# Chunks of 4096 rows with three buffers, evictions on ScalarE alone, weights in halves and a split store, in a 1x1 depthwise-separable convolution

## The chip, the cores and the metric

The kernel runs on one core of a Trainium2 chip. The metric is the time of one execution on the device in microseconds (us). The kernel before was timed nine times: median 589.32 us, lowest 587.19, highest 592.49.

## The reference

The input x is (1, 384, 384, 384) bf16: 147,456 pixels of 384 channels. With a depthwise kernel of size 1 the convolution is a scale of each channel, and the pointwise part is a 384 x 384 matrix product:

```python
def reference(x, dw, pw):          # dw: (1, 1, 384), pw: (384, 384)
    out = x * dw[0, 0]
    return jnp.einsum('bhwc,cd->bhwd', out, pw)
```

The kernel folds dw into the rows of pw once and then computes x times that matrix. Input and output are 113.2 MB each.

## The kernel before, in words

The pixels are 147,456 rows. 512 rows make a supertile, of which there are 288, and some supertiles make a chunk: 1, 1, 2, then 70 chunks of 4 (`LMAX`), then 2, 1, 1 (`_chunks`). A chunk is what one load or one store moves. In a chunk of L supertiles each of the 128 partitions holds 4 L consecutive rows, so a load has one contiguous run of 3072 L bytes per partition, 12 KB for L = 4. The store has four runs of 768 L bytes per partition, 3 KB for L = 4, because a quarter q of each supertile's rows comes out together. There are four X buffers (`NX`) and four O buffers (`NO`).

A supertile passes through these steps:

- VectorE (DVE) transposes it (L174). Two bf16 channels are taken as one 32-bit word, and 32 x 32 blocks are transposed, in two instructions: h = 0 for channels 0 to 191, h = 1 for the others. The result is T, in two buffers that alternate with the supertile's number.
- TensorE (PE) computes it in 48 matmuls (L134): 6 blocks b of channels, 2 parities `par`, and 4 row groups q of 32 partitions, which run side by side on the array. Each has 32 x 128 stationary values from T and streams 384 columns of the scaled weights w_r. The four q have a PSUM bank each, and PS has two sets of four, s = 0 and 1.
- The evictions go from PSUM to O as bf16: three of the four banks by ScalarE (ACT) in one instruction (L215), the fourth by VectorE (L212).
- The store goes out when the chunk is evicted.

The PE instructions are a loop of 144 passes, two supertiles each. The first matmul of a supertile waits until ACT has emptied its banks, that of q = 3 until VectorE has; each half waits for its transposes (L133 and the loop around it), and each finished half counts up `s_pe`, which the evictions and the next transposes into the same T wait for. VectorE's order is: eviction of supertile jj, then the transposes of jj + 2.

All loads and stores of x and out are issued by SyncE (SP) in one queue: first the loads of the first four chunks, then for each t load t + 4 (L95, waits until the last transpose of chunk t has read its X buffer) and store t (L105 and L107, wait for both evictions of its last supertile). An eviction into an O buffer in use waits for that store (L210, L211).

At the start ACT and SP issue dw, the first chunk and four copies of pw, one for each 32 partitions (L89). VectorE spreads dw over the partitions as dwsel (L186), transposes supertile 0, and then VectorE and ACT scale six slices of pw each, giving w_r (L197, L199). PE starts when all twelve are there. Two memsets and two tiny copies set the semaphores of the PSUM banks to "free".

Of the kernel before, what the change touches and what calls it, by code (L numbers as in the profile page):

```python
# [7 lines left out]
BF16 = mybir.dt.bfloat16  # L8
F32 = mybir.dt.float32
U32 = mybir.dt.uint32  # L10
COPY = mybir.ActivationFunctionType.Copy

LMAX = 4
NX = 4
NO = 4


def _chunks(n_super: int):

    head, tail = [1, 1, 2], [2, 1, 1]  # L20
    mid = n_super - sum(head) - sum(tail)
    assert mid > 0 and mid % LMAX == 0
    return head + [LMAX] * (mid // LMAX) + tail


@with_exitstack
def kernel(
# [11 lines left out]
    nc = tc.nc  # L39
    P = nc.NUM_PARTITIONS  # L40
    B, H, W, C = x.shape
    assert dw.shape[0] == 1 and dw.shape[1] == 1, "only k=1 depthwise supported"
    D = pw.shape[1]
    N = B * H * W
    assert C == 384 and D == 384 and N % 1024 == 0
    NB = C // 64

    xf = x.rearrange("b h w c -> (b h w) c")
    of = out.rearrange("b h w d -> (b h w) d")

    NS = N // 512
    chunks = _chunks(NS)
    NT = len(chunks)
    s0 = [sum(chunks[:t]) for t in range(NT)]

    consts = ctx.enter_context(tc.tile_pool(name="consts", bufs=1))
# [3 lines left out]
    pw_r = consts.tile([P, NB, 2, D], BF16, name="pw_r")  # L60
    w_r = consts.tile([P, NB, 2, D], BF16, name="w_r")
    dwt = consts.tile([32, NB, 2], BF16, name="dwt")
    dwsel = consts.tile([P, NB * 2], F32, name="dwsel")
    warm = consts.tile([P, 3], F32, name="warm")
    seed = consts.tile([P, 2], F32, name="seed")

    Xs = [bufp.tile([P, 4 * LMAX, C], BF16, name=f"X{i}") for i in range(NX)]
    Ts = [bufp.tile([P, NB, 256], BF16, name=f"T{i}") for i in range(2)]
    Os = [bufp.tile([P, 4 * LMAX * D], BF16, name=f"O{i}") for i in range(NO)]
# [3 lines left out]
    s_t = [[nc.alloc_semaphore(f"s_t{i}{h}") for h in range(2)] for i in range(2)]  # L73
    s_pe = nc.alloc_semaphore("s_pe")
    s_a = [nc.alloc_semaphore(f"s_a{i}") for i in range(2)]
    s_d = [nc.alloc_semaphore(f"s_d{i}") for i in range(2)]
    s_o = [nc.alloc_semaphore(f"s_o{i}") for i in range(NO)]
    s_dw = nc.alloc_semaphore("s_dw")
    s_pw = nc.alloc_semaphore("s_pw")
    s_ds = nc.alloc_semaphore("s_ds")  # L80
    s_wr = nc.alloc_semaphore("s_wr")
    s_seed = nc.alloc_semaphore("s_seed")

    with tc.tile_critical():  # L84
        pw_v = pw.rearrange("(b w r) d -> w b (r d)", w=32, r=2)
        dw_v = dw.rearrange("a e (b w r) -> w (a e b) r", w=32, r=2)

        def load_pw(eng, q):
            eng.dma_start(pw_r[32 * q : 32 * q + 32].rearrange("w b r d -> w b (r d)"), pw_v).then_inc(s_pw, 16)  # L89

        def load_x(t):
            L = chunks[t]
            r = 512 * s0[t]
            src = xf[r : r + 512 * L, :].rearrange("(p s) c -> p (s c)", p=P)
            d = nc.sync.dma_start(Xs[t % NX][:, : 4 * L, :].rearrange("p s c -> p (s c)"), src)  # L95
            if t >= NX:
                je = s0[t - NX] + chunks[t - NX] - 1
                d._wait_ge(s_t[je % 2][1], je // 2 + 1)
            d.then_inc(s_x[t % NX], 16)

        def store(t):
            L = chunks[t]
            r = 512 * s0[t]
            je = s0[t] + L - 1
            nc.sync.wait_ge(s_d[je % 2], je // 2 + 2)  # L105
            dst = of[r : r + 512 * L, :].rearrange("(q p j) d -> p q (j d)", q=4, p=P)
            d = nc.sync.dma_start(dst, Os[t % NO][:, : 4 * L * D].rearrange("p (q e) -> p q e", q=4))  # L107
            d._wait_ge(s_a[je % 2], je // 2 + 2)
            d.then_inc(s_o[t % NO], 16)


        nc.scalar.dma_start(dwt[:], dw_v).then_inc(s_dw, 16)
        load_x(0)
        load_pw(nc.scalar, 2)
        load_pw(nc.sync, 0)
        load_pw(nc.scalar, 3)
        load_pw(nc.sync, 1)
        for t in range(1, NX):
            load_x(t)
        for t in range(NT):  # L120
            if t + NX < NT:
                load_x(t + NX)
            store(t)
        for o in range(NO):
            nc.sync.wait_ge(s_o[o], 16 * len(range(o, NT, NO)))


        def supertile(s, rv):
            for b in range(NB):
                for par in range(2):  # L130
                    for q in range(4):
                        if par == 0 and q == 0 and b in (0, 3):
                            nc.tensor.wait_ge(s_t[s][b // 3], rv)  # L133
                        mm = nc.tensor.matmul(  # L134
                            PS[s][:, q, :D],
                            lhsT=Ts[s][32 * q : 32 * q + 32, b, par::2],
                            rhs=w_r[32 * q : 32 * q + 32, b, par, :],
                            start=(b == 0 and par == 0),
                            stop=(b == NB - 1 and par == 1),
                            tile_position=(32 * q, 0),  # L140
                        )
                        if b == 0 and par == 0 and q == 0:
                            mm._wait_ge(s_a[s], rv)
                        elif b == 0 and par == 0 and q == 3:
                            mm._wait_ge(s_d[s], rv)
                        if b in (2, 5) and par == 1 and q == 3:
                            mm.then_inc(s_pe)

        nc.tensor.wait_ge(s_wr, 2 * NB)
        with nc.tensor.Fori(0, NS // 2, 1) as it:  # L150
            rv = nc.tensor.to_reg(it + 1)
            for s in range(2):
                supertile(s, rv)


        for s in range(2):
            nc.vector.memset(seed[:, s : s + 1], 0.0).then_inc(s_d[s])  # L157
        nc.gpsimd.memset(warm[:], 0.0).then_inc(s_seed)  # L158
        for s in range(2):
            c = nc.scalar.copy(warm[:, s + 1 : s + 2], warm[:, 0:1])  # L160
            if s == 0:
                c._wait_ge(s_seed, 1)
            c.then_inc(s_a[s])

        def transposes(t, j):
            jj = s0[t] + j
            L = chunks[t]
            s = jj % 2
            Xw = Xs[t % NX][:].bitcast(U32)[:, : 4 * L, :].rearrange("p (k l) c -> p k l c", l=L)
            Tw = Ts[s][:].bitcast(U32).rearrange("p b (i k) -> p b k i", k=4)  # L170
            for h in range(2):
                if h == 0 and j == 0:
                    nc.vector.wait_ge(s_x[t % NX], 16 * (t // NX + 1))
                ins = nc.vector.transpose(  # L174
                    out=Tw[:, 3 * h : 3 * h + 3],
                    in_=Xw[:, :, j, 96 * h : 96 * h + 96].rearrange("p k (b w) -> p b k w", w=32),
                )
                if jj >= 2:
                    ins._wait_ge(s_pe, 2 * (jj - 2) + h + 1)
                ins.then_inc(s_t[s][h])  # L180

        order = [(t, j) for t in range(NT) for j in range(chunks[t])]

        nc.vector.wait_ge(s_dw, 16)
        for q in range(4):
            nc.vector.tensor_copy(  # L186
                dwsel[32 * q : 32 * q + 32, :], dwt[:].rearrange("w b r -> w (b r)")
            ).then_inc(s_ds)
        transposes(*order[0])
        for b in range(NB):  # L190
            for r in range(2):
                eng = nc.vector if r == 0 else nc.scalar
                if b == 0:
                    eng.wait_ge(s_pw, 64)  # L194
                sc = dwsel[:, 2 * b + r : 2 * b + r + 1]
                if r == 0:
                    i = nc.vector.tensor_scalar_mul(w_r[:, b, r, :], pw_r[:, b, r, :], sc)  # L197
                else:
                    i = nc.scalar.activation(w_r[:, b, r, :], pw_r[:, b, r, :], COPY, scale=sc)  # L199
                if b == 0:  # L200
                    i._wait_ge(s_ds, 4)
                i.then_inc(s_wr)
        transposes(*order[1])

        for jj, (t, j) in enumerate(order):
            L = chunks[t]
            s = jj % 2
            Ov = Os[t % NO][:, : 4 * L * D].rearrange("p (q j d) -> p q j d", q=4, d=D)
            if j == 0 and t >= NO:
                nc.vector.wait_ge(s_o[t % NO], 16 * (t // NO))  # L210
                nc.scalar.wait_ge(s_o[t % NO], 16 * (t // NO))  # L211
            e = nc.vector.tensor_copy(Ov[:, 3, j, :], PS[s][:, 3, :D])  # L212
            e._wait_ge(s_pe, 2 * jj + 2)
            e.then_inc(s_d[s])
            a = nc.scalar.copy(Ov[:, 0:3, j, :], PS[s][:, 0:3, :D])  # L215
            a._wait_ge(s_pe, 2 * jj + 2)
            a.then_inc(s_a[s])
            if jj + 2 < NS:
                transposes(*order[jj + 2])


# [28 lines left out]
```

## Time and profile before

| what | value |
|---|---|
| median of nine runs | 589.32 us |
| profiled execution, time in all | 587.68 us |
| its span, first to last instruction | 585.9 us |
| PE busy | 563.3 us (96%) |
| DVE busy | 564.0 us (96%) |
| ACT busy | 326.7 us (56%) |
| share of the 16 DMA engines taken by SP's queue | 98.6% |
| moved | 227.81 MB, 389 GB/s over the span |
| granted TensorE clock, mean | 0.995 |
| share of the chain that ended last: PE, DMA, ACT | 93%, 4%, 1% |

The profile is one execution. Times in views of it count from the span's start. A line like L134 is a line of the kernel. "Idle before" is time in which an engine had nothing running before an instruction, put down to what released it. A transfer's time "to landing" runs from its issue to the last of the semaphore marks that its DMA engines leave, so it contains the time in which it waits behind earlier transfers.

### The profile page before, as it was taken

What the parts mean: (1) busy time and instruction counts of PE and PEld (TensorE: products, weight loads), DVE (VectorE), ACT (ScalarE), POOL (GpSimd) and SP (SyncE); (2) the same over time, 40 slices, a digit from 0 to 9 for tenths busy, and PEclk for the clock granted to TensorE, in tenths of its full rate; (3) what the DMA queues carried; (4) which work ended last, traced back from release to release, by engine and by line L of the source; (5) the groups of instructions that cost most, each with busy time, mean ns of one, the idle gap of its engine ahead of it and who ended that gap; (6) DMA issues with size and microseconds to landing.
All of it is one profiled execution on the core that took longest, in us unless ns stands there. A gap on an engine that the chain in (4) does not pass through costs nothing.

```text
span 585.9 us, 30055 instructions
## 1 busy us (share of the span) xinstructions
PE 563.3 (96%) x13824; PEld 384.9 (66%) x13824; DVE 564.0 (96%) x876; ACT 326.7 (56%) x297; POOL 0.3 (0%) x5
## 2 busy tenths in 40 slices
PE   1999999999999999999999999999999999999993
PEld 0666666666666666666666666666666666666662
DVE  3899999999999999999999999999999999999993
ACT  3555555555565656565555555555555555555552
POOL 0000000000000000000000000000000000000000
PEclk9999999999999999999999999999999999999997
DMA  8999999999999999999999999999999999999965
GB/s 284 361 414 417 412 398 391 396 397 395 408 415 403 395 403 411 398 393 407 403 407 410 412 408 393 390 403 415 407 401 390 402 384 392 419 392 387 388 243 211
DMA packets 52126, 227.81 MB, mean 389 GB/s; under 512 B 2704, under 2 KB 6544, under 8 KB 43152
## 3 DMA queue, kind: packets, MB, share of 16 engines
q1 hardware_dynamic: 51488, 227.09, 98.6%
q10 hardware_dynamic: 624, 0.59, 0.4%
q14 instruction: 13, 0.11, 0.0%
q8 instruction: 1, 0.02, 0.0%
HBM read 114.43 MB, written 113.25 MB: 389 GB/s over the span
## 4 chain that ended last, share of the span: by engine, by line
PE 93%; DMA 4%; ACT 1%; SPq 0%; issue 0%; ACTq 0%
PE ps L134 93%; DMA out_dram<-O 3%; DMA pw_r<-in_pw_dram 1%; ACT w_r L199 1%; ACT O L215 0%; SPq L89 0%; SPq L95 0%; SPq L245 0%; ACTq L211 0%; ACTq L194 0%; SPq L84 0%
## 5 line engine op out<-in xcount | busy, mean ns | idle before, releaser
L134 PE MATMUL ps<-w_r,T 32*128 32x384 bf16 x13824 | 563.3, 322 | 13.1 <-ACT w_r L199 13.1
L134 PEld LDWEIGHTS ps<-w_r,T 32*128 32x128 bf16 x13824 | 384.9, 93 | 191.1 <-issue 13.1
L215 ACT CAST O<-ps 128x1152 bf16<-128x1152 f32 x288 | 322.0, 1118 | 243.2 <-PE ps L134 242.0
L174 DVE STREAM_TRANSPOSE T<-X 128x384 uint32<-128x384 uint32 x576 | 449.6, 858 | 0.0
L212 DVE CAST O<-ps 128x384 bf16<-128x384 f32 x288 | 160.7, 558 | 6.1 <-PE ps L134 4.2
L199 ACT ACTIVATE w_r<-pw_r,dwsel 128x384 bf16<-128x384 bf16 x6 | 3.1, 603 | 5.8 <-DMA pw_r<-in_pw_dram 5.8
L186 DVE CAST dwsel<-dwt 32x12 f32<-32x12 bf16 x4 | 0.7, 164 | 3.8 <-DMA dwt<-in_dw_dram 3.7
L197 DVE TENSOR_SCALAR w_r<-pw_r,dwsel 128x384 bf16<-128x384 bf16 x6 | 1.5, 314 | 2.5 <-DMA pw_r<-in_pw_dram 2.5
L160 ACT ACT_TABLE_LOAD x1 | 1.3, 1283 | 2.3 <-issue 2.3
L157 DVE MEMSET seed<- 128x1 f32 x2 | 0.1, 59 | 1.0 <-SPq L84 1.0
L160 ACT COPY warm<-warm 128x1 f32<-128x1 f32 x2 | 0.3, 189 | 0.0
L234 POOL MEMSET const-bfloat16-1.0<- 128x1 bf16 x1 | 0.1, 101 | 0.0
L234 POOL MEMSET const-uint8-127<- 128x1 uint8 x1 | 0.1, 101 | 0.0
L158 POOL MEMSET warm<- 128x3 f32 x1 | 0.1, 100 | 0.5 <-SPq L84 0.5
L234 POOL MEMSET const-float32-0.0<- 128x1 f32 x1 | 0.1, 98 | 0.2 <-issue 0.2
L234 POOL MEMSET const-float32-1.0<- 128x1 f32 x1 | 0.1, 98 | 0.0
## 6 DMA issues: line engine op xcount, KB each, us to landing
X<-in_x_dram SPq DMA_DIRECT2D x70, 1536.0 KB, 13.7
out_dram<-O SPq DMA_DIRECT2D x70, 1536.0 KB, 15.3
X<-in_x_dram SPq DMA_DIRECT2D x4, 384.0 KB, 10.8
X<-in_x_dram SPq DMA_DIRECT2D x2, 768.0 KB, 14.0
out_dram<-O SPq DMA_DIRECT2D x4, 384.0 KB, 7.1
out_dram<-O SPq DMA_DIRECT2D x2, 768.0 KB, 9.6
pw_r<-in_pw_dram ACTq DMA_DIRECT2D x2, 288.0 KB, 6.1
pw_r<-in_pw_dram SPq DMA_DIRECT2D x2, 288.0 KB, 6.7
```

The costliest lines, as they stand in the source:

```text
L134: mm = nc.tensor.matmul(PS[s][:, q, :D], lhsT=Ts[s][32 * q : 32 * q + 32, b, par::2], rhs=w_r[32 * q : 32 * q + 32, b, par, :], start=(b = ...
L157: nc.vector.memset(seed[:, s : s + 1], 0.0).then_inc(s_d[s])
L158: nc.gpsimd.memset(warm[:], 0.0).then_inc(s_seed)
L160: c = nc.scalar.copy(warm[:, s + 1 : s + 2], warm[:, 0:1])
L174: ins = nc.vector.transpose(out=Tw[:, 3 * h : 3 * h + 3], in_=Xw[:, :, j, 96 * h : 96 * h + 96].rearrange("p k (b w) -> p b k w", w=32),)
L186: nc.vector.tensor_copy(dwsel[32 * q : 32 * q + 32, :], dwt[:].rearrange("w b r -> w (b r)")).then_inc(s_ds)
L197: i = nc.vector.tensor_scalar_mul(w_r[:, b, r, :], pw_r[:, b, r, :], sc)
L199: i = nc.scalar.activation(w_r[:, b, r, :], pw_r[:, b, r, :], COPY, scale=sc)
L212: e = nc.vector.tensor_copy(Ov[:, 3, j, :], PS[s][:, 3, :D])
L215: a = nc.scalar.copy(Ov[:, 0:3, j, :], PS[s][:, 0:3, :D])
L234: nc = _bacc.Bacc("TRN2", target_bir_lowering=False, num_devices=1)
```

## The change

- `LMAX` goes from 4 to 8, and X and O have three buffers each instead of four. The chunks become 1, 1, 2, 2, 3, 3, 4, then 32 of 8, then 6, 4, 3, 2, 1. A full chunk's load has runs of 24 KB, its store runs of 6 KB.
- In every fourth full chunk (t = 9, 13, ... 37) the store is issued as four transfers: partitions 0 to 111, 112 to 118, 119 to 125 and 126 to 127.
- ACT evicts all four banks (L256 of the changed kernel), and VectorE none, except in the very last supertile, where each takes two banks, and SP and ACT store one half each. The matmul of q = 3 no longer waits for VectorE, and the two memsets go.
- The weights are loaded in eight transfers, blocks 0 to 2 of all partitions first, then 3 to 5. dwsel is made by ACT. VectorE scales nine of the twelve slices, ACT three (par = 1 of b = 0, 2, 4). PE no longer waits for all twelve: in supertiles with s = 0 the first matmul of each (b, par) waits for its own slice.
- Before its first supertile PE runs 88 matmuls on a tile of zeros, which POOL fills; their result is overwritten.

```diff
-LMAX = 4
-NX = 4
-NO = 4
+LMAX = 8
+NX = 3
+NO = 3
...
-    head, tail = [1, 1, 2], [2, 1, 1]
+    head, tail = [1, 1, 2, 2, 3, 3, 4], [6, 4, 3, 2, 1]
...
+        parts = {t: [(0, P)] for t in range(NT)}
+        for t in range(NT):
+            if chunks[t] == LMAX and t % 4 == 1:
+                parts[t] = [(0, 112), (112, 119), (119, 126), (126, 128)]
...
-            nc.sync.wait_ge(s_d[je % 2], je // 2 + 2)
             dst = of[r : r + 512 * L, :].rearrange("(q p j) d -> p q (j d)", q=4, p=P)
-            d = nc.sync.dma_start(dst, Os[t % NO][:, : 4 * L * D].rearrange("p (q e) -> p q e", q=4))
-            d._wait_ge(s_a[je % 2], je // 2 + 2)
-            d.then_inc(s_o[t % NO], 16)
+            src = Os[t % NO][:, : 4 * L * D].rearrange("p (q e) -> p q e", q=4)
+            nc.sync.wait_ge(s_a[je % 2], je // 2 + 2)
+            for lo, hi in parts[t]:
+                nc.sync.dma_start(dst[lo:hi], src[lo:hi]).then_inc(s_o[t % NO], 16)
...
         load_x(0)
-        load_pw(nc.scalar, 2)
-        load_pw(nc.sync, 0)
-        load_pw(nc.scalar, 3)
-        load_pw(nc.sync, 1)
+        for h in range(2):
+            for q in range(2):
+                load_pw(nc.scalar, 2 + q, h)
+                load_pw(nc.sync, q, h)
         for t in range(1, NX):
             load_x(t)
-        for t in range(NT):
+        for t in range(NT - 1):
             if t + NX < NT:
                 load_x(t + NX)
             store(t)
+        nc.sync.dma_start(of_last[:, 2:4], o_last[:, 2:4])._wait_ge(s_d, 1).then_inc(
+            s_last, 16
+        )
...
+        wr_eng = {(b, r): int(r == 1 and b % 2 == 0) for b in range(NB) for r in range(2)}
...
                         if b == 0 and par == 0 and q == 0:
                             mm._wait_ge(s_a[s], rv)
-                        elif b == 0 and par == 0 and q == 3:
-                            mm._wait_ge(s_d[s], rv)
+                        elif s == 0 and q == 0:
+                            mm._wait_ge(*wr_done[b, par])
...
-        nc.tensor.wait_ge(s_wr, 2 * NB)
+        nc.tensor.wait_ge(s_zero, 1)
+        with nc.tensor.Fori(0, 11, 1) as _:
+            for i in range(8):
+                nc.tensor.matmul(
+                    PS[1][:, i % 4, :D],
+                    lhsT=zero[32 * (i % 4) : 32 * (i % 4) + 32, 0:P],
+                    rhs=zero[32 * (i % 4) : 32 * (i % 4) + 32, :],
+                    start=True,
+                    stop=True,
+                    tile_position=(32 * (i % 4), 0),
+                )
+        nc.tensor.wait_ge(*wr_done[0, 0])
...
-        nc.vector.wait_ge(s_dw, 16)
+        nc.scalar.wait_ge(s_dw, 16)
         for q in range(4):
-            nc.vector.tensor_copy(
-                dwsel[32 * q : 32 * q + 32, :], dwt[:].rearrange("w b r -> w (b r)")
-            ).then_inc(s_ds)
+            nc.scalar.copy(dwsel[32 * q : 32 * q + 32, :], dwt[:].rearrange("w b r -> w (b r)")).then_inc(s_ds)
...
-            e = nc.vector.tensor_copy(Ov[:, 3, j, :], PS[s][:, 3, :D])
-            e._wait_ge(s_pe, 2 * jj + 2)
-            e.then_inc(s_d[s])
-            a = nc.scalar.copy(Ov[:, 0:3, j, :], PS[s][:, 0:3, :D])
+            nq = 4
+            if jj + 1 == NS:
+                nq = 2
+                nc.vector.wait_ge(s_o[t % NO], o_count[t % NO][t // NO])
+                e = nc.vector.tensor_copy(Ov[:, nq:4, j, :], PS[s][:, nq:4, :D])
+                e._wait_ge(s_pe, 2 * jj + 2)
+                e.then_inc(s_d)
+            a = nc.scalar.copy(Ov[:, 0:nq, j, :], PS[s][:, 0:nq, :D])
             a._wait_ge(s_pe, 2 * jj + 2)
             a.then_inc(s_a[s])
             if jj + 2 < NS:
                 transposes(*order[jj + 2])
+        nc.scalar.dma_start(of_last[:, 0:2], o_last[:, 0:2])._wait_ge(s_a[(NS - 1) % 2], (NS - 1) // 2 + 2).then_inc(
+            s_last, 16
+        )
```

## The prediction, made before the changed kernel was run

> **What bounds the kernel now.** I read four views: the page's groups of instructions, the chain that ended last, the transfers by window, and the busy table of chosen windows. First the groups (line, engine, operation, tiles, shape, count; then busy us, mean ns of one, idle us before them and who ended it):
>
> ```profile
> L134 PE MATMUL ps<-w_r,T 32*128 32x384 bf16 x13824 | 563.3, 322 | 13.1 <-ACT w_r L199 13.1
> L215 ACT CAST O<-ps 128x1152 bf16<-128x1152 f32 x288 | 322.0, 1118 | 243.2 <-PE ps L134 242.0
> L174 DVE STREAM_TRANSPOSE T<-X 128x384 uint32<-128x384 uint32 x576 | 449.6, 858 | 0.0
> L212 DVE CAST O<-ps 128x384 bf16<-128x384 f32 x288 | 160.7, 558 | 6.1 <-PE ps L134 4.2
> ```
>
> PE and VectorE both look full. The start times decide. Matmuls start in groups of four every 162.5 ns, 12 groups a supertile, and supertiles 1.950 us apart, at every percentile from the 5th to the 99th, with no longer step where a wait stands (b = 0, b = 3). ACT and DVE evictions start within 0.01 us of each other, so both are released by PE. VectorE fits (0.48 us from eviction to transposes, 1.48 us back) with nothing spare, but PE never waits for it. So between the second supertile and the last PE sets a pace that no edit here changes: 288 x 1.950 = 561.6 us. Time can be won only before and after it. The chain shows both (start us, us, what):
>
> ```profile
> 1.89 7.70 DMA pw_r<-in_pw_dram
> ...
> 9.67 3.15 ACT w_r L199 x6
> ...
> 13.15 547.73 PE ps L134 x12779
> ...
> 562.04 14.82 DMA out_dram<-O
> ...
> 576.93 1.12 ACT O L215
> ```
>
> Head: the weights land at 9.58, ACT scales its six slices, PE starts at 13.15. Its first 10 groups take 320 ns, the others 162.5: 10 x 157.5 ns = 1.5 us lost, and the second supertile starts at 16.62, the third at 18.57. Tail: the last matmul ends at 576.44 and the span at 585.9, so 9.5 us follow; a store that took 14.82 us delays the last eviction by some 0.4 us of them. That store needs explaining. Time from issue to landing, from 100 to 150 us and then from 500 to 550:
>
> ```profile
> out_dram<-O SPq DMA_DIRECT2D x7, 1536.0 KB, 11.7
> X<-in_x_dram SPq DMA_DIRECT2D x6, 1536.0 KB, 10.5
> ```
>
> ```profile
> out_dram<-O SPq DMA_DIRECT2D x7, 1536.0 KB, 21.2
> X<-in_x_dram SPq DMA_DIRECT2D x5, 1536.0 KB, 20.1
> ```
>
> The same transfers take 9.5 us longer. Each leaves 16 landing marks, one per DMA engine. For the store issued at 109.6 us the 15th mark came after 11.3 us and the last after 11.4; for that of 538.6, after 11.4 and 21.7. One engine lags by 10.3 us in 430, 2.4%; fifteen keep up. The busy table at the end (window, length, PE, PEld, DVE, ACT, POOL, granted clock, DMA share, GB/s) shows it alone:
>
> ```profile
> 567.50:569.80 2.30, 2.30 (x67) 1.58 (x60) 2.30 (x4) 1.47 (x2) 0.00 (x0) 1.00 0.06 23
> 580.80:584.50 3.70, 0.00 (x0) 0.00 (x0) 0.00 (x0) 0.00 (x0) 0.00 (x0) 0.50 0.06 22
> ```
>
> A share of 0.06 is 1 of 16. The last store, issued at 578.08, had 15 marks by 580.68 and the 16th at 584.55: 3.9 us of the span are this engine's.
>
> [...]
>
> **The change part by part.**
>
> *Head.* DVE loses the dwsel copies (4.84 to 5.59), so its first transposes start when chunk 0 lands, 5.06 instead of 5.61, and end near 6.6. The weights come in halves. Chunk 0 and the first half are as many bytes as chunk 0 and the first two of four weight loads before, whose marks were complete at 7.16; I take 7.2. ACT, after its table load and warm copies (done 3.91, now 0.9 later for two more DMA issues), waits for dwt (4.81) and makes four small copies (164 ns each on DVE, 189 ns for the nearest ACT copy, so 0.7 to 0.8 us): 5.6, hidden behind 7.2; behind that wait stand only ACT's own slices. DVE then makes four slices (0.24 us apart) and ACT two (0.52 apart), and the first half of supertile 0 is through by about 8.8. The second half of the weights lands when all did, about 9.6. DVE makes five slices, 9.6 + 5 x 0.24 + 0.1 = 10.9, and supertile 0 ends near 11.3. DVE's next transposes run 10.9 to 12.5, their first half ready at 11.8, so supertile 1 runs 11.8 to 13.75. From there the pace is 1.950. Supertile 2 starts at 13.75 instead of 18.57: **-4.8 us**. The 88 warm matmuls are 22 groups: 3.6 us all warm, 7.0 all cold. Begun near 1.3 us (the POOL memset that PE waits for is larger than any shown; 0.1 to 1 us), they end by 8.3 to 9.2 at the latest, and PE has to wait for the second half until 9.6 anyway: nothing on the path. If they didn't warm the clock, only what lies behind 10.9 would pay, up to 1.5 us.
>
> *Three X buffers, finer first chunks.* SP issues load t+3 before store t, so load 4 is queued behind store 0, which waits for the eviction of supertile 0 (13.1). At the 786 KB per 1.9 us that chunk 2 took (10.33 to 12.23), load 3 lands at 14.1 and load 4, behind store 0, at 17.9; PE would starve only if load 4 came after 20.7. Carried on the same way, chunk 7 lands at 36.9 against 40.2. Nothing on the path, margins 2.8 and 3.3 us.
>
> *Eviction on ACT alone.* 1536 elements instead of 1152: at least 1118 ns, pro rata 1491. [...] It starts 0.22 us after PE leaves the bank and PE wants it back after 1.95[...]. DVE falls from 1.95 to about 1.5 us a supertile. Neither is on the path. The 11 new waits in each loop pass are satisfied ones, like those of b = 3, which cost 0 to 1 ns.
>
> *Longer runs.* A 3072-byte packet has a median of 121 ns, 6144 one of 234, 12288 one of 460: about 8 ns fixed and 36.8 ns per 1024 bytes. An engine needs 2 x 460 + 8 x 121 = 1888 ns for a supertile now, and 912 + 4 x 234 = 1848 with 24 KB and 6 KB: 2.1% less. An unseen 24 KB packet could also be no cheaper per byte: 0 to 2.1%.
>
> *The split store.* [...] The three more issues cost SP 3 x 0.39 us a chunk, with SP idle most of each 15.6 us.
>
> *Tail.* PE ends 4.8 us earlier, 571.6. The last eviction is halved[...]. The stores before it are queued: 768 KB took 3.5 to 3.7 us from issue on fifteen engines, so chunk 42, issued near 571.3, lands near 574.9 and the last 384 KB about 1.0 us later, 575.9. From the last landing to the end it was 1.35 us. End 577.3: after PE's last matmul 5.7 instead of 9.5, **-3.8 us**.
>
> *Sum.* 585.9 - 4.8 - 3.8 = 577.3 us. The profiled execution took 587.68 in all, 1.8 around its span: 579.1. It lies 1.6 below the median of the nine runs (589.32); the full 8.6 off that median gives 580.7. Part of the spread of those runs (587.19 to 592.49) should be the lagging engine's, which goes, so I choose **579.5**.
>
> **The rivals.** *The lag stays* (the slow engine is fed as before or its packets gain nothing): PE is not touched, since a load may now take 31.2 us (two chunks of 15.6) and takes under 30, but the tail keeps its 3.9 us: 579.5 + 4 = 583.5. For it: the cause of the slowness isn't seen. *The early start is given back*: with 4 supertiles in three buffers at the start instead of 8 in four, a load misses its time and PE pauses for what was won: 579.5 + 4.8 = 584.3, at most 588. For it: margins under 3.5 us, in a stretch at full DMA rate. Against: the trace's first loads came in at 414 GB/s. *Slower*: [...] A load has 31.2 us of room and takes about 11 without lag, so PE stalls from a lag of 20 us on, that is above an excess of 3.8%[...].
>
> **How the numbers follow.** Forecast 0.70; lag stays 0.13; start given back 0.08 (0.05 still faster, 0.03 within the bound); something that cancels all 0.01; slow engine loaded more 0.08. About 0.3% is what a measurement of this kernel can tell from no change. So faster 0.88, same 0.04, slower 0.08. The range runs from 577 (tail or warm start 2.5 us better) to 586 (both mild rivals, each with some spread), which leaves about 0.15 outside.
>
> **What would show it.** Right: PE's second loop supertile starting near 12, all later ones 1.950 apart; [...]landing times of full-chunk loads flat from 100 to 550 us; all 16 marks of the last store within 0.5 us; 5.7 us after the last matmul. Wrong: PE pauses before 45 us that end on X; landing times that grow; ACT's eviction over 1.7 us, from which PE would wait for PSUM in every supertile.

## The result, and the profile after

The changed kernel takes 622.49 us (median of ten runs, 615.41 to 636.13) against 589.49 us before (31 runs): 1.0526 times as long, 95% interval 1.0491 to 1.0561, which compares undisturbed runs only. I had forecast 579.5 us and a range up to 586. The profiled execution has a span of 621.7 us, 35.8 more than before.

First the groups of the page after, in the columns of the prediction:

```profile
L162 PE MATMUL ps<-w_r,T 32*128 32x384 bf16 x13824 | 572.5, 324 | 33.5 <-ACT O L256 31.0
L213 DVE STREAM_TRANSPOSE T<-X 128x384 uint32<-128x384 uint32 x576 | 503.1, 878 | 105.2 <-PE ps L162 34.9
L256 ACT CAST O<-ps 128x1536 bf16<-128x1536 f32 x288 | 412.6, 1437 | 192.3 <-PE ps L162 148.1
```

The eviction takes 1437 ns, inside the forecast's bounds (1118 at least, 1491 pro rata). But PE now sits idle for 31.0 us behind ACT, and its matmuls are busy 572.5 us instead of 563.3. The waits of the same kernel (engine, line, releaser: us in total, times, longest) say why:

```profile
ACT O L256 <- DMA out_dram<-O: 44.1, 14, 8.0
PE ps L162 <- ACT O L256: 31.0, 12, 7.1
DVE T L213 <- DMA X<-in_x_dram: 19.7, 6, 5.6
```

ACT waits for O buffers whose stores haven't landed, and PE for ACT. The busy table by stage (window, length, PE, PEld, DVE, ACT, POOL, granted clock, DMA share, GB/s) puts all of PE's idle time into the second half:

```profile
14.00:320.00 306.00, 306.00 (x7540) 226.56 (x7533) 275.11 (x316) 225.92 (x157) 0.00 (x0) 1.00 1.01 407
320.00:613.00 293.00, 261.41 (x6192) 164.23 (x6184) 223.49 (x256) 184.47 (x129) 0.00 (x0) 0.97 0.89 336
```

Until 320 us PE never stops. From 355 us on it does, about once a chunk. The chain that ended last, which was PE's for 547.73 us in one piece before, is now broken by stores (start us, us, what):

```profile
12.10 325.86 PE ps L162 x8016
...
393.85 35.05 DMA out_dram<-O
...
443.87 41.29 DMA out_dram<-O
...
500.13 42.00 DMA out_dram<-O
```

One place in the timeline (start us, us, instruction, idle before):

```profile
443.87 0.38 SPq L124 DMA_DIRECT2D out_dram<-O  x1
451.88 2.78 ACT L256 CAST O<-ps 128x1536 bf16<-128x1536 f32 x2 [8.03 <-DMA out_dram<-O]
453.37 0.14 PEld L162 LDWEIGHTS ps<-w_r,T 32*128 32x128 bf16 x8 [7.50 <-ACT O L256]
453.37 1.15 PE L162 MATMUL ps<-w_r,T 32*128 32x384 bf16 x12 [7.11 <-ACT O L256]
```

ACT may not evict into its next O buffer for 8.03 us. PE's two sets of banks are then full and it stops for 7.11; the supertile after the pause takes 3.81 us instead of 1.95: the granted clock is 0.50 from 451 to 457 us and 1.00 again from 458.

The 35.8 us, from the start times of the matmuls, are three terms. Supertile 2 starts at 14.04 instead of 18.57: -4.5. From there to the last supertile the starts lie 41.8 us further apart than 1.950 each. After the last matmul 7.9 us follow instead of 9.5: -1.5. The sum is 35.8. The 41.8 are 31.6 us in which PE stands still and some 10 of slow matmuls.

The time to landing of the loads, here those issued from 110 to 140 us and then those of 3072 KB from 500 to 540, has grown as that of the kernel before did, but further:

```profile
X<-in_x_dram SPq DMA_DIRECT2D x2, 3072.0 KB, 18.9
```

```profile
X<-in_x_dram SPq DMA_DIRECT2D x1, 3072.0 KB, 31.2
```

The landing marks show how. From here on the *lag* of a transfer is the time from its issue to its last mark, and the *slow engine* is the one that leaves that mark. The loads of full chunks, in the changed kernel (issue time; us from issue to the 8th, 15th and last mark):

```
issue at   8th   15th   last
  85.4    14.5   15.6   17.5
 101.0    15.3   19.1   20.0     split store issued at 89.8
 147.8    12.5   17.1   18.9
 163.4    13.0   20.7   22.3     split store at 152.2
 210.2    11.3   19.4   20.1
 225.8    11.2   23.6   24.4     split store at 214.6
 288.2    12.1   24.8   26.7     split store at 277.0
 319.4    11.5   22.9   26.8
 335.0    11.4   23.6   32.9     (split store at 339.4)
 439.4    11.2   18.8   37.3
```

Half of the engines keep landing after 11 to 15 us. The last falls behind in steps, from 17.5 to 37.3 us, and the steps lie at the split stores; between them the lag mostly stays or shrinks. At 32.9 us it is past the two chunks (31.2 us) that a buffer gives. The load issued at 335.0 goes into the queue 4.4 us ahead of the split store of 339.4, and still its lag is 6.1 us longer than that of the load before it. Up to some 370 us the 15th mark is late too, so more than one engine lags; in the profiled run of e2 it comes after 12 to 18 us.

### The profile page after: what moved, and what is told of

Its sections match the earlier page's. It is cut to its first block, busy times and chain, and to the rows that moved or that the text cites. A ratio compares the mean times of both kernels' runs of the same rounds, so it can differ in the third digit from the quotient of the medians.

```text
span 621.7 us, 29865 instructions
## 1 busy us (share of the span) xinstructions
PE 578.9 (93%) x13912; PEld 397.2 (64%) x13912; DVE 506.2 (81%) x586; ACT 416.7 (67%) x298; POOL 0.5 (0%) x6
## 4 chain that ended last, share of the span: by engine, by line
PE 61%; DMA 32%; SPq 3%; ACT 3%; DVE 0%; issue 0%; ACTq 0%; DVEq 0%
PE ps L162 61%; DMA out_dram<-O 30%; SPq L124 3%; ACT O L256 3%; DMA pw_r<-in_pw_dram 1%; SPq L92 0%; DVE w_r L234 0%; DVE O L253 0%; DVE T L213 0%; SPq L100 0%; ACTq L248 0%; SPq L289 0%; DVEq L252 0%; SPq L86 0%
## 5 line engine op out<-in xcount | busy, mean ns | idle before, releaser
L162 PE MATMUL ps<-w_r,T 32*128 32x384 bf16 x13824 | 572.5, 324 | 33.5 <-ACT O L256 31.0
L213 DVE STREAM_TRANSPOSE T<-X 128x384 uint32<-128x384 uint32 x576 | 503.1, 878 | 105.2 <-PE ps L162 34.9
L256 ACT CAST O<-ps 128x1536 bf16<-128x1536 f32 x288 | 412.6, 1437 | 192.3 <-PE ps L162 148.1
L162 PEld LDWEIGHTS ps<-w_r,T 32*128 32x128 bf16 x13824 | 393.7, 94 | 212.3 <-ACT O L256 36.9
L181 PE MATMUL ps<-zero 32*128 32x384 bf16 x88 | 6.4, 473 | 1.4 <-POOL zero L197 1.4
L181 PEld LDWEIGHTS ps<-zero 32*128 32x128 bf16 x88 | 3.5, 130 | 3.9 <-issue 1.6
L236 ACT ACTIVATE w_r<-pw_r,dwsel 128x384 bf16<-128x384 bf16 x3 | 1.7, 610 | 2.6 <-DMA pw_r<-in_pw_dram 2.6
```

Of the source, the lines that this page charges most:

```text
L162: mm = nc.tensor.matmul(PS[s][:, q, :D], lhsT=Ts[s][32 * q : 32 * q + 32, b, par::2], rhs=w_r[32 * q : 32 * q + 32, b, par, :], start=(b = ...
L181: nc.tensor.matmul(PS[1][:, i % 4, :D], lhsT=zero[32 * (i % 4) : 32 * (i % 4) + 32, 0:P], rhs=zero[32 * (i % 4) : 32 * (i % 4) + 32, :], s ...
L213: ins = nc.vector.transpose(out=Tw[:, 3 * h : 3 * h + 3], in_=Xw[:, :, j, 96 * h : 96 * h + 96].rearrange("p k (b w) -> p b k w", w=32),)
L256: a = nc.scalar.copy(Ov[:, 0:nq, j, :], PS[s][:, 0:nq, :D])
```

## The experiments

My theory after this comparison (A): the split gives more bytes to the slow engine. Rivals: three buffers of 8 supertiles with long runs are too much for the DMA (B); a store in pieces collides with other transfers, whoever gets the bytes (C).

### e1: every store whole

```diff
-                parts[t] = [(0, 112), (112, 119), (119, 126), (126, 128)]
+                parts[t] = [(0, P)]
```

> The changed kernel with every store in one transfer of 128 partitions. Theory A (the split store feeds the DMA engine that is already slow: its last landing mark trailed the eighth by 3 to 4 us more after each split store, and stayed level over the chunks between): no stall of PE after the first supertile, pace 1.950 us throughout, 578 to 583 us, ratio about 0.985. Theory B (three buffers of 8 supertiles and long runs are what the DMA cannot keep up with): landing times still grow to over 30 us and the time stays at 610 to 625 us.

Measured: 578.51 us (four runs, 578.37 to 580.39), ratio 0.9852, interval 0.9829 to 0.9875. B is out: the rest of the change is worth -1.5%, and the split store alone turns it into +5.3%. Two of the groups and the second stage of this kernel:

```profile
L162 PE MATMUL ps<-w_r,T 32*128 32x384 bf16 x13824 | 562.4, 321 | 2.3 <-DVE w_r L234 1.8
L256 ACT CAST O<-ps 128x1536 bf16<-128x1536 f32 x288 | 413.5, 1436 | 148.8 <-PE ps L162 148.8
```

```profile
320.00:570.00 250.00, 250.00 (x6163) 183.94 (x6156) 224.27 (x255) 184.47 (x129) 0.00 (x0) 1.00 0.97 387
```

From supertile 2 on PE loses 0.1 us in all, and ACT waits for PE alone. The last mark of the loads is 17.1 us after issue at 69 us and 19.0 at 490. The chain ends as I had worked it out (start us, us, what):

```profile
11.30 559.97 PE ps L162 x13776
571.27 0.02 issue
571.29 0.96 DVE O L253
```

### e2: the same stores as 112 and 16 partitions

```diff
-                parts[t] = [(0, 112), (112, 119), (119, 126), (126, 128)]
+                parts[t] = [(0, 112), (112, 128)]
```

> The changed kernel with the split stores as 112 and 16 partitions[...]. Theory A (who gets the bytes): like the whole store, 578 to 584 us. Theory C (a store in pieces, [...]is slow by itself): 600 us or more, with landing times that step up after each split store.

Measured: 613.6, 615.74, 618.49 and 578.17 us. Three of four runs are about as slow as the changed kernel; in the profiled one (613.6) the last mark of the loads is 19.0 us after issue at 272 us and 30.4 at 335. If 112 and 16 partitions go evenly to 16 engines (my estimate, from the 16 marks that a transfer leaves; no trace shows it), each gets 7 + 1, as many as the 8 of a whole store. As far as that holds, this speaks against A and for C. The run without loss has no trace; what spared it is open.

### e3: the kernel before with the split

```diff
+        parts = {t: [(0, P)] for t in range(NT)}
+        for t in range(NT):
+            if chunks[t] == LMAX and t % 4 == 1:
+                parts[t] = [(0, 112), (112, 119), (119, 126), (126, 128)]
...
+            for lo, hi in parts[t]:
+                nc.sync.dma_start(dst[lo:hi], src[lo:hi]).then_inc(s_o[t % NO], 16)
...
```

> The kernel before with the split of the changed kernel on every fourth full chunk (18 of 70), nothing else changed. Theory A: [...]its lag passes the slack of four small X buffers in the second half and PE stalls: 595 to 615 us. Theory B: the split relieves the slow engine or does nothing: 585 to 590 us.

Measured: 621.06 us, ratio 1.0563 (1.0545 to 1.0582). More than I expected. The split needs nothing else of the change to do its harm. Its waits:

```profile
ACT O L225 <- DMA out_dram<-O: 63.3, 35, 3.8
DVE O L222 <- DMA out_dram<-O: 25.7, 34, 2.4
```

The kernel before had 1.3 and 1.8 us there, once each.

### e4: which engine is the slow one

The kernel before, with two stores in pieces:

```diff
...
+        parts[60] = [(0, 112), (112, 119), (119, 123), (123, 128)]
+        parts[66] = [(0, 112), (112, 118), (118, 121), (121, 123), (123, 128)]
...
```

> The kernel before, with two late stores in pieces as a probe: chunk 60 as 112, 7, 4 and 5 partitions, chunk 66 as 112, 6, 3, 2 and 5. The lagging engine leaves its landing marks last, one for each piece that it takes part in[...]. Time as before, 586 to 592 us.

Measured: 592.31 us in one run (587.93 for the kernel before on the same chip). Of chunk 60's store 29 engine marks came by 487.26 us and three at 496.96, 497.52 and 498.05; of chunk 66's the last three came at 546.90, 547.45 and 547.98, 10 us after the others. If late marks are the slow engine's, it takes part in three of the four pieces of the one store and in three of the five of the other; which ones, and which number the engine has, isn't shown. In the changed kernel three marks of the split store issued at 484 us came late, at 522.88, 523.93 and 524.99; so did three of e11's second split store (366.73, 367.79 and 368.82), on another chip. The steps of 1.03 to 1.06 us are about four packets at the pace of this engine (8.39 us for a whole store in e1, a sixteenth of whose 512 packets is 32, so 0.26 each), and a partition has four. So I estimate one partition more in each of two small pieces: 9 with the 7 of an even share of 112, where an even share of a whole store is 8. I had counted on the split to relieve this engine.

### e5: two transfers of 128 partitions

```diff
-        parts = {t: [(0, P)] for t in range(NT)}
+        parts = {t: [(0, 4)] for t in range(NT)}
...
-                parts[t] = [(0, 112), (112, 119), (119, 126), (126, 128)]
+                parts[t] = [(0, 2), (2, 4)]
...
-                nc.sync.dma_start(dst[lo:hi], src[lo:hi]).then_inc(s_o[t % NO], 16)
+                nc.sync.dma_start(dst[:, lo:hi], src[:, lo:hi]).then_inc(s_o[t % NO], 16)
```

> The changed kernel with the split stores cut into quarters 0-1 and quarters 2-3, each transfer over all 128 partitions. Theory C ([...]the slow store packets, 440 to 1100 ns instead of 234, came only in stores over fewer than 128 partitions): no store packets over 300 ns before the tail, lag as with whole stores, 578 to 581 us. Theory D (a store in two transfers is slow by itself): slow packets and 600 us or more.

Measured: 578.91 us, ratio 0.9835 (0.9808 to 0.9861), last mark 18.7 us after issue at 70 us and 20.0 at 475. The second transfer costs nothing (578.51 us in e1). It is the partitions that matter, as the times of single packets in the trace show. Packets of 6144 bytes (the stores of full chunks) that start between 60 and 525 us, median 234 ns in all kernels, and the split stores whose packets fall into that stretch:

```
kernel                       split stores   of 400 ns or more   of 800 or more
e1  whole stores                   0                3                  0
e5  two of 128 partitions          7                3                  0
changed kernel                     7              308                 40
e2  112 + 16                       7              350                 41
e7  112 alone                      7              309                 32
e11 changed, two chunks            2               76                 16
e10 112 alone                     14              689                 78
e6  64 + 64                        7              708                 10
```

Some 38 to 50 long packets go with each store that has a 112-partition piece (a whole store has 512 packets), next to none with the others of 128. In the changed kernel 146 of the 308 last 446 to 474 ns, that is 1.9 to 2.0 times 234, and ten about 879, 3.8 times. What makes them long is not shown: the trace has no engine numbers, and no run shows how a piece of 112 partitions is dealt out.

### e6: 64 and 64 partitions

```diff
-                parts[t] = [(0, 112), (112, 119), (119, 126), (126, 128)]
+                parts[t] = [(0, 64), (64, 128)]
```

> The changed kernel with the split stores as partitions 0-63 and 64-127. Theory C: [...]nearly all its packets take about twice 234 = 470 ns and the store 7.5 us more on every engine; per four chunks of 62.4 us the DMA then needs about 59 + 7.5 us, so PE stalls: 600 to 625 us. Without collisions: 578 to 582 us and packets of 234 ns.

Measured: 579.87 us, one run, no stall. The direction was right, the size wrong: of 3584 packets in seven such stores 645 took 400 to 520 ns. The excess over 234 ns is 191 us more than in e1, over 16 engines and 7 stores 1.7 us each instead of 7.5. At the first of them the 8th mark goes from 14.5 to 19.6 us and the last from 17.6 to 21.9; both come down again, and later splits add less (23.0 us after issue at 163, 21.1 at 194). Why most packets keep their length here is open, and as long as it is, this run speaks against C as I had put it: pieces of fewer than 128 partitions alone don't make the loss.

### e7: 112 partitions alone

```diff
-                parts[t] = [(0, 112), (112, 119), (119, 126), (126, 128)]
+                parts[t] = [(0, 112)]
```

> The changed kernel with only partitions 0-111 of the split stores written; the last 16 partitions of 8 of the 44 chunks are left out of the output. It tells which piece collides. If only the small pieces do: all store packets at 234 ns and no lag added, 578 to 580 us. If the 112-partition piece collides too: packets of about 446 ns[...] in it; each engine has 7/8 of the packets, so the lag grows less than with all pieces and the time lies at 578 to 590 us.

Measured: 591.01 us, one run, with PE stalls from 479 us. There is less to store than in e1, for the slow engine too by the times below (7.38 us for its share of a split, 8.39 for that of a whole store), and it still falls behind: 17.8 us (issue at 194), 19.2, 20.2, 21.6, 23.0 after each further split, and 29.1 at 475. So A can't be the main cause: an eighth less to store, and the lag grows. The 112-partition piece alone is enough; the small pieces seem to add to it (615 to 636 us with them).

Where the time goes can be read from the distance of last marks. In the changed kernel the last marks of loads and stores come in the order of issue, from first to last (0.89 to 14.09 us apart), so I take the time from one last mark to the next as what the later transfer cost the slow engine (us; "ahead of" means the last whole store and the last load issued before the split store):

```
                                      store   load
e1, full chunks, usual                 8.39   7.24
e7, its share of the split at 214.1     9.44
e7, ahead of the split at 463.7       13.58   8.49
e7, its own share of that split        7.38
e10, ahead of the split at 276.8      13.59   8.75
e10, its own share of that split       7.52
changed, ahead of the split at 339.4  12.38   9.36
changed, its share of that split       9.33
```

With whole stores in e1 the slow engine needs 8.39 + 7.24 = 15.63 us for a chunk, and PE's pace is 15.60: it has nothing spare. What it loses falls on the transfer that it is at when the others move the pieces. Early in e7 that is its own share, 9.44 us where 7/8 of 8.39 would be 7.34 (estimated). Later it is further behind; then its own share costs no more than that (7.38), and the loss lies in transfers issued before the split store. The long packets of the table under e5 start just then: in the changed kernel from 348.4 to 357.7 us, while the slow engine is at the store ahead of the split from 346.1 to 358.5.

### e8: whole stores, small chunks

```diff
-LMAX = 8
-NX = 3
-NO = 3
+LMAX = 4
+NX = 4
+NO = 4
...
-    head, tail = [1, 1, 2, 2, 3, 3, 4], [6, 4, 3, 2, 1]
+    head, tail = [1, 1, 2, 2, 3, 3, 4], [4, 4, 3, 2, 2, 1]
...
-                parts[t] = [(0, 112), (112, 119), (119, 126), (126, 128)]
+                parts[t] = [(0, P)]
```

> The changed kernel with whole stores, but chunks of 4 supertiles and four buffers as before: early start, eviction on ACT and finer tail stay, the 24 KB and 6 KB runs go. If the longer runs are what stops the slow engine's lag: its last mark falls behind again by about 10 us from 100 to 550 us as in the kernel before, the tail stays long, 581 to 585 us. If the lag has another cause (evictions, order of the queue): flat landing times and 578 to 580 us.

Measured: 581.08 us, ratio 0.9877 (0.985 to 0.9904). As expected, the slow engine falls behind again, here the loads issued from 110 to 140 us and from 500 to 540:

```profile
X<-in_x_dram SPq DMA_DIRECT2D x4, 1536.0 KB, 13.0
```

```profile
X<-in_x_dram SPq DMA_DIRECT2D x3, 1536.0 KB, 20.1
```

After its last matmul 8.2 us follow, 5.3 in e1. PE ends within 0.1 us of e1, so the longer runs, with the chunk list and the buffers that go with them, are worth their 2.8 us in the tail alone.

### e9: without the warm-up

The 88 matmuls on zeros and their wait go from e1.

```diff
-        with nc.tensor.Fori(0, 11, 1) as _:
-            for i in range(8):
-                nc.tensor.matmul(
...
```

> Whole stores in one transfer, and the 88 matmuls on zeros taken out. As I predicted, the weights are late enough to hide the warm-up, and without it supertile 0 runs at the slow clock: 10 groups at 320 instead of 162.5 ns cost 1.5 us at most, of which the wait for the second half of the weights hides a part: supertile 2 starts 0.3 to 1.5 us later than with the warm-up (13.25 us), 578.5 to 580.2 us. If the clock takes longer to come up because PE pauses between slices: 2 us or more.

Measured: 579.02 us, ratio 0.9829 (0.9793 to 0.9865), which can't be told from e1. In the traces supertile 2 starts at 14.38 instead of 13.25 us, 1.1 later, within what I expected; but the second half of the weights also landed 0.56 us later than in e1 (9.68 against 9.12), so about half of it is left for the warm-up.

### e10: 112 partitions in every second full chunk

```diff
-            if chunks[t] == LMAX and t % 4 == 1:
-                parts[t] = [(0, 112), (112, 119), (119, 126), (126, 128)]
+            if chunks[t] == LMAX and t % 2 == 1:
+                parts[t] = [(0, 112)]
```

> As the run that writes only partitions 0-111 of the split stores, but in every second full chunk instead of every fourth; the last 16 partitions of 16 chunks are left out of the output, so there is 6% less to store. Theory C[...]: the lag steps up twice as often, PE stalls from the first half on, 600 to 625 us although less is moved. Theory A (bytes per engine decide): each engine has 6% less to store, 577 to 580 us.

Measured: 642.2 us, one run, above what I expected. Moving less costs 64 us against e1: bytes per engine are not the cause. Nor is it the issuing by SP: no transfer between 60 and 540 us took it more than 0.40 us to issue. The stalls come from 293 us on at every second chunk, as often as the split stores; they are 5.8 to 7.8 us between two supertiles and 3.3 to 3.8 in the next.

```profile
ACT O L256 <- DMA out_dram<-O: 56.4, 13, 6.6
```

### e11: two splits only

```diff
-            if chunks[t] == LMAX and t % 4 == 1:
+            if chunks[t] == LMAX and t in (9, 25):
```

> The changed kernel with the four-part store in two chunks only (t = 9 and t = 25) instead of eight. If what decides is whether the slow engine's lag passes the 31 us that two chunks give a load: each split adds 3 to 6 us to 18, so it ends near 25 to 28 us, no stall of PE, 578 to 582 us. If a split costs PE time directly (the 33 us of the change over 8 splits, some 4 to 5 us each): 586 to 589 us.

Measured: 589.26 us, one run. The time is about the one that I gave for a direct cost, but not the course. The lag of the loads is 18.1 us before the first split, 20.6 after it and level to 21.1 for 220 us; after the second it is 25.7. PE runs at 1.950 us through both. Then, with no further split, the lag creeps on, 25.8 to 29.6 us from 380 to 490, and PE stalls from 464 us, over 100 us after the last split:

```profile
ACT O L256 <- DMA out_dram<-O: 10.0, 6, 3.6
PE ps L162 <- ACT O L256: 4.1, 3, 2.7
```

So a split costs lag and no PE time, as I expected, but in this run a lag of 25.8 us didn't stay where it was. By the distance of last marks the slow engine's stores from 397 us on cost 8.4 us as before, its loads 7.5 to 8.0 instead of 7.24.

## Why the prediction was wrong, by its own steps

- *PE sets the pace, only head and tail can be won.* Right for the kernel before and for e1. It overlooked that a late DMA can take the pace away (PE 31.0 us idle behind ACT, ACT 44.1 behind stores).
- *Head, -4.8.* Measured -4.5 in the changed kernel and -5.3 in e1 (supertile 2 at 14.04 and 13.25; I had 13.75). The weights' halves landed at 7.53 and 9.91 us in the changed kernel instead of 7.2 and 9.6, and at 6.89 and 9.12 in e1, so the difference between the two is that of the weights.
- *Three buffers and finer first chunks.* Right in the end, not in its margins (2.8 and 3.3 us). Load 4 landed at 20.71, its limit was 20.7, and chunk 7 at 39.44 against 40.2. PE kept its pace there in the changed kernel; in other runs (e2, e5, e7, e9, e11) it lost 0.1 to 0.5 us before supertile 6, the first of chunk 4.
- *Eviction on ACT.* 1436 to 1437 ns; with whole stores PE never waits for it.
- *Longer runs, 0 to 2.1%.* The 24 KB packet has a median of 912 ns, exactly the estimate (its 36.8 ns are per 1000 bytes, not per 1024). In e1 the last mark slips by 2 us in 420 (0.5%) where it slipped by 2.4%.
- *Tail.* In e1 5.3 us after the last matmul (I had 5.7); the last eviction took 957 ns on DVE.
- *Split store.* This is the step that failed. I priced it as a move of bytes that relieves the slow engine, with three cheap issues. That it gets less was an assumption, which no trace had shown, and both halves were wrong. By the late marks under e4 it gets more, 9 partitions for 8 by my estimate. And above all the cost isn't in bytes: while a store with a piece of 112 partitions is moved, 38 to 50 packets take 400 ns or more instead of 234, and in the cases shown under e7 the slow engine loses 4 to 5 us on the store that it still has to do and 1 to 2 on the load. e7 and e10 give it less and it falls behind all the same, while in e5, with two transfers but all partitions in each, it does not. I had put this at nothing; between the profiled executions of e1 and the changed kernel it is 45.1 us of span (576.6 and 621.7).

Without that step the sum was right: 577.3 us of span forecast, 576.6 in e1. In part that is luck: the head came out 0.5 us better than forecast with early weights, and the lag stayed nearly flat through the longer runs alone, without the help of the split that I had counted in.

My slower rival had the course right (a lagging engine, a lag past the room of two chunks, PE stalled), but it put the lag down to extra bytes; the runs show long packets. I gave it 0.08.

That the slow engine loses its time while the others move the pieces, later on in transfers ahead of the split, is shown by the distances under e7, if the last mark is always that engine's; that it has nothing spare to recover with, too (15.63 us for a chunk of 15.60). Not shown is the step between: why packets get long then. The ninth partition, by the estimate under e4, adds some 1 us a split (9.33 against 8.39 us under e7); how much of the loss that makes is open, and e2, without it if its pieces are dealt evenly, was at 614 to 618 in three runs. Open are also why one engine is slow at all, why a split costs it more later on (in e7 1 to 2 us of lag at the splits from 214 to 401 us, 6.5 at that of 463.7), and why its loads slow down in e11 with no new split beside them.

## What to carry to other kernels

Read the landing marks of each transfer one by one: the median time to landing and a DMA share near 1 hid that one of 16 engines was at its limit (15.63 us for a chunk of 15.60 in e1). Where that is so, cut a transfer along the free dimension (the elements within a partition) and keep all 128 partitions in each piece (e5, 578.91 us against 578.51 whole; e7, with partitions 0 to 111, took 591.01), and don't count on moving work between engines by partition counts without measuring packet times. Here a lag was free at first (e11: PE at 1.950 us up to a lag of 25.7 us, stalls on its way from there to 29.6), so a change can look harmless for half a run.

## What I had not expected of the hardware

- One DMA engine needs more time than the rest: alone at the end of the kernel before, its 3072-byte packets took 135 ns and started every 132, while the median packet of the run took 121. In e1 it is slower in the stores alone: 8.39 us for a store, a sixteenth of whose 512 packets would take 7.5 at the median of 234 ns, but 7.24 for a load, a sixteenth of whose 128 would take 7.3 at 912.
- While that engine lags, SP's issue of a small piece can take long: the first 7-partition piece issued at 484.68 us in the changed kernel took 7.32 us to issue instead of 0.39, and the load behind it went out at 497.68.
- PE's clock falls back in one pause: after the 7.1 us that end at 453 us the granted clock was 0.50 and the next supertile took 3.81 us, much as the first one at the start (3.47 us in the kernel before).
